# A gated linear recurrence and a max-out layer on one core: w_out loaded two rows to a partition, unit 0's gates in halves of heads, decays from sums of row pairs

## The chip, the core and the metric

The kernel runs on one core of a Trainium2 chip. The core has a matrix engine (TensorE, PE; its weight loads are listed apart as PEld), a vector engine (VectorE, DVE), a scalar engine (ScalarE, ACT), a general engine (GpSimd, POOL) and an engine that issues transfers (SyncE, SP). Each works through its own list of instructions in order and waits on semaphores. SBUF holds tiles of 128 partitions; PSUM has eight banks that TensorE writes. Times are device microseconds of one run.

## The reference

```
_attn: batch, n_heads, seq, head_dim = 4, 8, 768, 48
for t in range(S):
    state = alpha[:, :, t, :, None] * state + k[:, :, t] (outer) v[:, :, t]
    y[:, :, t] = q[:, :, t] @ state
x = y, heads side by side              # 3072 rows x 384
h1, h2 = x @ w1, x @ w2                # 384 x 1024 each
out = maximum(h1, h2) @ w_out          # 1024 x 384
```

All inputs and the output are fp32. Alpha lies between 0.8 and 1.0.

## The kernel before

**Units.** The 4 x 768 positions are cut into 12 units of 256 positions: unit u is batch u % 4, and its place in the sequence is u // 4. A unit has two chunks of 128 positions. `load(u)` brings alpha, k, q and v in; `gla(u)` computes the recurrence of the unit; `moe(u)` computes the layer behind it.

**The recurrence by chunks.** `ln` (ACT) takes the logarithm of alpha into `lg`, two positions (r = 0, 1) to a partition. `sums` (TensorE) multiplies `lg` by triangular matrices, which gives running sums within a chunk (`cs`, one PSUM bank to a chunk). For units 2 to 11 these matmuls use half of the array's rows ("tiled" in the plan); for units 0 and 1, the `TWO` units, they use full matrices `ti` and `ts`. `exps` has three parts: eight small TensorE matmuls per unit (`e_de`, line 494) that sum `lg` over groups of 32 partitions with the indicator `ind4`, for decays of whole half-chunks and chunks; exponentials of minus the sums (`em`, line 499) and of the sums (in place, line 501); and the exponential of the decays (`de`, line 504). `prep` multiplies k by `em` on POOL (`kn`, line 540) and q by the other on DVE (`qn`, line 542), and transposes both on TensorE (line 550, copied out as `qk` by DVE, line 558). `chunk` makes the scores (`e_p`, line 641, also tiled), masks them on DVE (`pt`, line 663), forms the new state `tm` (DVE, line 624) from k-v products (line 612), scales the former state by the decays into `sb` (POOL, line 599), and computes y from both (`e_y`, lines 672 and 675). y is copied out (`yc`, ACT, line 683), transposed (line 689) and stored as `xt` (DVE).

**The layer.** Instead of max(x w1, x w2) it computes x w2 + max(x (w1 - w2), 0). `weights` subtracts the weights on DVE (`w12`, line 439, four slices g of 256 columns) and casts `w_out` to `wo` (line 444; slices 0 and 1 on ACT, 2 and 3 on POOL). `w2_rows` casts w2 (`w2h`, ACT, line 412), transposes it and multiplies it by `wo` into `w2o` (line 429, 24 matmuls), so that x w2 w_out becomes one product with a 384 x 384 matrix. `moe(u)` makes four hidden products (`e_h`, line 729, one PSUM bank each), takes their ReLU into `gt` (ACT, line 740; for f2 = 1 from unit 3 on by DVE, line 737), and adds the output products (`e_o`, line 760) of `xt` with `w2o` and of `gt` with `wo`.

**The order of the work.** `Plan` is a list scheduler that runs while the program is built. Every step is given to it with an engine, a planned duration, what it reads and writes, and a key; PSUM banks are assigned on the way. At each planned moment an engine takes the ready step with the lowest key. The keys are ten times the unit plus offsets; `OFF0` shifts them for units 0 and 1. The resulting order of each engine is then fixed in the program. A change of one duration or key therefore can move other steps. Where the plan expects TensorE to be without work in the first 40 us, filler matmuls on `wsrc` (line 450) are placed.

**Transfers.** All loads are issued by SP in the order of `HEAD` and then unit by unit:

```
HEAD = 'k0 a0 a1 q0 v0 k1 q1 w20 w22 w21 v1 wo0 wo1 wo2 wo3 w11 w10 w13 w12'
```

Here `a0` is alpha of unit 0, `w20` is row block 0 of w2, `wo0` is slice 0 of w_out and `w11` is slice 1 of w1. The outputs are stored by ACT's queue.

Of the kernel before, what the change touches and what calls it, by code (L numbers as in the profile page):

```python
# [196 lines left out]
LATE = 2.5
# [5 lines left out]
JOIN_PP = -50  # L203
CS_UP = 2
RING = 3
OFF = {}
OFF0 = {'DVE:xt': -3.0, 'DVE:pt': -15.7, 'PE:op': 8.8, 'PE:hp': -8.2, 'ACT:yc': -9, 'PE:x': 6.7}
HEAD = 'k0 a0 a1 q0 v0 k1 q1 w20 w22 w21 v1 wo0 wo1 wo2 wo3 w11 w10 w13 w12'


# [1 line left out]
def kernel(  # L212
# [29 lines left out]
    def sbt(name, shape, dt, n=1):  # L242
        return [constp.tile(shape, dt, name=f"{name}{i}") for i in range(n)]
# [61 lines left out]
    add("DVE", c_warm, 0.25, writes=["wsrc"], key=-9)  # L305
    nc.scalar.preload_act_table_set("natural_log_exp_and_others")
    for i in range(2):
        add("DVE", lambda i=i: nc.vector.memset(LG[i], 0.0), 0.35, writes=[("lg", i)], key=-8)

    def c_t2():  # L310
        nc.gpsimd.memset(t2, 1.0)
# [58 lines left out]
    for i in range(4):  # L370
        add("DVE", lambda i=i: nc.vector.memset(SB[i], 0.0), 0.2, writes=[("sb", i)], key=-4)


    def load(u, what="akqv"):
        n, (b, cp) = u % NLD, (u % B, u // B)
        t0 = 256 * cp
        lat = 2.5 + max(0.0, min(LATE, LATE * (u - 1) / 3.0))
        ws = [({4: "w2f", 5: "w1f", 6: "wof"}[u], g) for g in range(3 if u == 4 else 4)] if u in (4, 5, 6) else []

        def pairs(dst, src, keys):  # L380
            add("SP", lambda: nc.sync.dma_start(  # L381
                out=dst.rearrange("p (h x) -> p h x", h=H),
                in_=src[b, :, t0 : t0 + 256, :].rearrange("h (p r) d -> p h (r d)", r=2)),
                1.26 if u in TWO else 1.5, writes=[*keys, *ws], key=-1, lat=lat)
# [15 lines left out]

    def load_w(m, g):
        fs = slice(256 * g, 256 * g + 256)
        if m == "2":
            dst, src, t = w2f[:, g, :], moe_w2[128 * g : 128 * g + 128, :], 1.36
        elif m == "1":
            dst, src, t = w1f[:, :, fs], moe_w1[:, fs].rearrange("(s p) f -> p s f", p=128), 1.15
        else:
            dst, src, t = wof[:, 2 * g : 2 * g + 2, :], moe_w_out[fs, :].rearrange("(s p) d -> p s d", p=128), 1.1
        add("SP", lambda: nc.sync.dma_start(out=dst, in_=src), t, writes=[(f"w{m}f", g)], key=-1, lat=2.5)  # L409

    def w2_rows(ds):
# [14 lines left out]
        y = f"wq{ds}"
        P.ps(y, 1, "w")
        for f in range(NF):
            add("PE", lambda f=f: nc.tensor.matmul(
                b32(y, DM), lhsT=w2T[:, f, 128 * ds : 128 * ds + 128], rhs=wo16[:, f, :],  # L430
                start=(f == 0), stop=(f == NF - 1)),
                0.162, reads=[("w2T", ds), ("wo16", f // 2)], writes=[y], key=KEY_WO)
        add("ACT", lambda: nc.scalar.copy(out=w2o[:, ds, :], in_=b32(y, DM)),
            0.38, reads=[y], writes=[("w2o", ds)], key=KEY_WO)

    def weights(g):
        fs = slice(256 * g, 256 * g + 256)
        eng, ns = ("POOL", nc.gpsimd) if g in W12_POOL else ("DVE", nc.vector)
        add(eng, lambda: ns.tensor_sub(out=w12[:, :, fs], in0=w1f[:, :, fs], in1=w2f[:, :, fs]),
            1.9 if g in W12_POOL else 0.95, reads=[("w1f", g), *(("w2f", ds) for ds in range(ND))],  # L440
            writes=[("w12", g)], key=KEY_W12)
        on = g in WO_ACT
        cp = nc.scalar.copy if on else nc.gpsimd.tensor_copy
        add("ACT" if on else "POOL", lambda: cp(  # L444
            out=wo16[:, 2 * g : 2 * g + 2, :], in_=wof[:, 2 * g : 2 * g + 2, :]),
            0.73 if on else 0.9, reads=[("wof", g)], writes=[("wo16", g)], key=KEY_W)
# [8 lines left out]
    def csv(u, i):  # L455
        return b32(("cs", u, i), DM).rearrange("p (h d) -> p h d", h=H)

    def ln(u):
        lg = LG[u % 2]
        add("ACT", lambda: nc.scalar.activation(  # L460
            out=lg[:, :, :, 0:D].rearrange("p r h d -> p h r d"), in_=AF[u % NLD], func=ACTF.Ln),
            0.82, reads=[("af", u % NLD)], writes=[("lg", u % 2)], key=10 * u)
        for i in range(2):
            P.ps(("cs", u, i), 1, "g")

    def e_cs(u):
        lg = LG[u % 2]
        if u in TWO:
            for i in range(2):
                for r in range(2):  # L470
                    nc.tensor.matmul(csv(u, i), lhsT=ts if r > i else ti, rhs=lg[:, r, :, 0:D],
                                     start=(r == 0), stop=(r == 1))
            return
        for r in range(2):
            for a in range(2):
                s = slice(64 * a, 64 * a + 64)
# [1 line left out]
                                 start=(r == 0), stop=(r == 1))  # L478

    def sums(u):  # L480
        by2 = u in TWO
        add("PE", lambda: e_cs(u), 0.65 if by2 else 0.33, reads=[("lg", u % 2), "tt" if by2 else "t2"],
            writes=[("cs", u, 0), ("cs", u, 1)], key=10 * u + (0 if by2 else CS_UP), tiled=not by2, join=10 * u + (0 if by2 else JOIN_CS))

    def exps(u):
        lg, de, k0 = LG[u % 2], DE[u % 8], 10 * u

        def dps():
            return bank(("cs", u, 0))[:, 384:400].rearrange("p (j m) -> p j m", j=HP)

        def e_de():
            for j in range(HP):
                for r in range(2):
                    nc.tensor.matmul(dps()[:, j, :], lhsT=pm(lg[:, r, 2 * j : 2 * j + 2, :]), rhs=ind4,  # L494
                                     start=(r == 0), stop=(r == 1))
        add("PE", e_de, 0.2, reads=[("lg", u % 2), "ind4"], writes=[("cs", u, 0)], key=k0)
        for i in range(2):
            em = (2 * u + i) % RING
            add("ACT", lambda i=i, em=em: nc.scalar.activation(out=EM[em], in_=csv(u, i), func=ACTF.Exp, scale=-1.0),  # L499
# [7 lines left out]
    def gla(u):  # L507
# [10 lines left out]
        if by2:  # L518
# [13 lines left out]
        def prep(i):  # L532
# [7 lines left out]
            add("POOL", lambda: nc.gpsimd.tensor_mul(out=kn[:, :, 0:D], in0=kin, in1=EM[m3]),  # L540
                0.95, reads=[*rk, ("em", m3)], writes=[("kn", m3)], key=kk)
# [33 lines left out]
        def chunk(a):  # L575
# [69 lines left out]
            elif a == 0:  # L645
# [204 lines left out]
```

## Time and profile before

| | us |
|---|---|
| median of 3 runs | 140.12 (139.96 to 141.34) |
| the profiled execution's own time | 140.14 |
| its span, first to last instruction | 138.0 |
| mean granted TensorE clock | 0.998 |
| TensorE busy | 132.0 |
| VectorE busy | 94.2 |
| ScalarE busy | 83.1 |
| GpSimd busy | 65.7 |
| bytes moved, in and out | 28.58 MB |

How the lines of the profile are read. In a timeline a line is a run of like instructions: start, time from the start of the first to the end of the last, engine, line of the code, operation, output <- input, shape, count, and in brackets the idle time of the engine before it and what ended that. Matmuls are pipelined, so the end of one lies after the start of the next; distances between starts say what a matmul costs. In a table by windows a line is a stretch, its length, the busy time of each engine with its instructions in brackets, TensorE's granted clock, the share of time in which the transfer engines were busy, and GB/s. In the row of slices each digit is the busy share of a fortieth of the span, in tenths.

### The profile page before, as it was taken

The numbers are of one execution on the slowest core, as the hardware profiler recorded it, in microseconds if no ns is written. First come the engines' busy times: TensorE is split into PE (matmuls) and PEld (weight loads), VectorE is DVE, ScalarE is ACT, GpSimd is POOL, SyncE is SP. The second block draws the span as 40 slices with busy tenths as digits, with TensorE's granted clock in tenths as the row PEclk, the third lists the DMA queues.
The fourth block names the chain that finished last, engine by engine and source line by source line (L and its number), as shares of the span: only waits on it lengthen the run. The fifth ranks groups of instructions, "written<-read, shape, count | busy, mean of one in ns | idle before, by whom it ended". The sixth has DMA issues, their size and how long they took to land.

```text
span 138.0 us, 4307 instructions
## 1 busy us (share of the span) xinstructions
PE 132.0 (96%) x1704; PEld 101.7 (74%) x1704; DVE 94.2 (68%) x199; ACT 83.1 (60%) x176; POOL 65.7 (48%) x127
## 2 busy tenths in 40 slices
PE   6698999999999999999999999999999999999991
PEld 6686985777768768678777877877777778687870
DVE  4936999932868847968977949948929759474300
ACT  3295895679364876565844845837737638245341
POOL 7458547206418159186482871844845817500000
PEclk9999999999999999999999999999999999999999
DMA  3999999989999999999989999999999130030113
GB/s 94 319 313 380 374 381 350 265 171 194 236 280 226 256 220 208 239 229 188 316 165 210 271 200 290 202 245 293 226 183 271 23 114 5 0 114 5 73 41 114
DMA packets 87427, 28.58 MB, mean 207 GB/s; under 512 B 81520, under 2 KB 86768, under 8 KB 87408
## 3 DMA queue, kind: packets, MB, share of 16 engines
q1 hardware_dynamic: 84240, 23.60, 72.9%
q10 hardware_dynamic: 3168, 4.72, 9.1%
q8 instruction: 13, 0.21, 0.6%
q14 instruction: 6, 0.05, 0.1%
HBM read 23.59 MB, written 4.72 MB: 205 GB/s over the span
## 4 chain that ended last, share of the span: by engine, by line
PE 79%; SPq 9%; DMA 6%; POOL 2%; issue 1%; ACT 0%; ACTq 0%
PE pb L760 31%; PE pb L729 23%; PE pb L550 6%; DMA ld<-in_moe_w_out_dram 6%; SPq L381 5%; PE pb L641 4%; SPq L409 4%; PE pb L675 3%; PE pb L689 3%; PE pb L477 3%; PE pb L672 3%; PE pb L612 2%; PE pb L494 2%; POOL sb L599 1%; POOL wo L444 1%
## 5 line engine op out<-in xcount | busy, mean ns | idle before, releaser
L760 PE MATMUL pb<-wo,gt 128*128 128x384 f16 (+2 forms) x200 | 39.1, 319 | 0.0
L540 POOL TENSOR_TENSOR kn<-ld,em 128x384 f16<-128x384 f32 x24 | 23.5, 1000 | 30.5 <-ACT em L499 26.7
L729 PE MATMUL pb<-xt,w 128*128 128x256 f16 x288 | 36.0, 272 | 0.0
L740 ACT ACTIVATE gt<-pb 128x512 f16<-128x512 f32 x39 | 23.1, 598 | 13.3 <-PE pb L729 12.2
L663 DVE TENSOR_TENSOR pt<-pb,u 128x512 f16<-128x512 f32 x48 | 29.8, 684 | 1.0 <-PE pb L641 0.7
L729 PEld LDWEIGHTS <-w 128*128 128x128 f16 x288 | 26.8, 98 | 3.7
L760 PEld LDWEIGHTS <-gt 128*128 128x128 f16 x200 | 17.7, 98 | 8.4
L599 POOL TENSOR_TENSOR sb<-tm,dd 64x192 f16<-64x192 f32 x40 | 20.7, 518 | 4.8 <-DVE tm L624 2.3
L768 ACT COPY os<-pb 128x384 f32<-128x384 f32 (+2 forms) x25 | 11.6, 468 | 18.8 <-PE pb L760 18.8
L558 DVE COPY qk<-pb 128x1024 f16<-128x1024 f16 x20 | 13.8, 691 | 11.6 <-ACT os L768 10.2
L542 DVE TENSOR_TENSOR qn<-ld,pb 128x384 f16<-128x384 f32 x24 | 12.4, 549 | 8.9 <-ACT pb L501 7.5
L760 PE MATMUL pb<-w2o,xt 128*128 128x384 f16 (+2 forms) x75 | 15.8, 319 | 0.0
L561 POOL CAST vc<-ld 128x384 f16<-128x384 f32 x20 | 10.0, 504 | 11.7 <-DMA ld<-in_v_dram 11.0
L499 ACT ACTIVATE em<-pb 128x384 f32<-128x384 f32 x24 | 10.8, 491 | 6.3 <-PE pb L477 6.3
L460 ACT ACTIVATE lg<-ld 128x768 f16<-128x768 f32 x12 | 10.2, 846 | 5.2 <-DVE qn L369 3.8
L683 ACT CAST yc<-pb 128x384 f16<-128x384 f32 x24 | 11.8, 491 | 2.5 <-PE pb L675 1.8
L698 DVE COPY xt<-pb 128x384 f16<-128x384 f16 x20 | 7.1, 356 | 6.8 <-PE pb L689 6.4
L624 DVE TENSOR_TENSOR tm<-pb,sb 64x192 f32<-64x192 f32 x32 | 11.3, 352 | 0.6
L675 PEld LDWEIGHTS <-pt 128*128 128x128 f16 x192 | 9.6, 96 | 2.2 <-issue 1.0
L450 PE MATMUL pb<-wsrc 128*128 128x128 f16 x125 | 9.9, 242 | 1.1 <-DVE wsrc L304 1.1
L501 ACT ACTIVATE pb<-pb 128x384 f32<-128x384 f32 x24 | 10.8, 489 | 0.0
L675 PE MATMUL pb<-vc,pt 128*128 128x48 f16 x160 | 9.6, 184 | 0.0
(79 smaller groups left out, 179.2 us busy)
## 6 DMA issues: line engine op xcount, KB each, us to landing
ld<-in_alpha_dram SPq DMA_DIRECT2D x12, 384.0 KB, 5.0
out_dram<-os ACTq DMA_DIRECT2D x11, 384.0 KB, 4.1
ld<-in_k_dram SPq DMA_DIRECT2D x20, 192.0 KB, 4.5
ld<-in_q_dram SPq DMA_DIRECT2D x20, 192.0 KB, 4.3
ld<-in_v_dram SPq DMA_DIRECT2D x20, 192.0 KB, 4.6
ld<-in_moe_w_dram SPq DMA_DIRECT2D x3, 512.0 KB, 6.1
ld<-in_moe_w_out_dram SPq DMA_DIRECT2D x4, 384.0 KB, 7.7
ld<-in_moe_w_dram SPq DMA_DIRECT2D x4, 384.0 KB, 8.3
```

Source lines behind the costliest of these rows:

```text
L540: add("POOL", lambda: nc.gpsimd.tensor_mul(out=kn[:, :, 0:D], in0=kin, in1=EM[m3]), 0.95, reads=[*rk, ("em", m3)], writes=[("kn", m3)], ke ...
L542: add("DVE", lambda: nc.vector.tensor_mul(out=qn[:, :, 0:D], in0=qin, in1=csv(u, i)), 0.5, reads=[*rq, ("cs", u, i)], writes=[("qn", m3)], ...
L558: add("DVE", lambda: nc.vector.tensor_copy(out=QK[m3], in_=b16(tp, 1024).rearrange("p (w j c) -> p w j c", w=2, j=HP)), 0.6, reads=[tp], w ...
L599: add("POOL", lambda r=r, e=e: nc.gpsimd.tensor_mul(out=sb[r, :, e], in0=TM[tmo][r], in1=dd[r, :].unsqueeze(2).to_broadcast([64, HP, D])), ...
L624: nc.vector.tensor_add(out=TM[tmi][r], in0=t[r, :, e], in1=sb[r, :, e])
L663: add("DVE", lambda e=e: nc.vector.tensor_mul(out=pt[:, e], in0=b32(pp[e], 512).rearrange("p (j c) -> p j c", j=HP), in1=uv.unsqueeze(1).t ...
L675: nc.tensor.matmul(t[:, 96 * j + D * e : 96 * j + D * e + D], lhsT=pt[:, e, j, :], rhs=vc[:, 2 * j + e, :], start=not has, stop=(e == 1) o ...
L683: add("ACT", lambda: nc.scalar.copy(out=yc, in_=b32(yp, DM)), 0.38, reads=[yp], writes=[("yc", ci % 2)], key=kk)
L729: nc.tensor.matmul(t[:, m, :], lhsT=w12[:, ds, f * 128 : f * 128 + 128], rhs=xt[:, ds].rearrange("p a c -> p (a c)"), start=(ds == 0), sto ...
L740: add("ACT", lambda g2=g2, v2=v2: nc.scalar.activation(out=g2, in_=v2(), func=ACTF.Relu), 0.48, reads=[x], writes=[("gt", u % 3, f2)], key ...
L760: nc.tensor.matmul(b32(x, c1 - c0), lhsT=l, rhs=r, start=first and y == 0, stop=last and y == len(ws) - 1)
L768: add("ACT", lambda m=m, x=x, c0=c0, c1=c1: nc.scalar.copy(out=os_[:, m, c0:c1], in_=b32(x, c1 - c0)), 0.06 + w / 1200.0, reads=[x], write ...
```

## The change

1. `w_out` is loaded with two neighbouring rows to a partition, so that a partition's part of a slice is one run of 3072 bytes and no longer two of 1536. This orders the hidden columns differently: column 256 g + 2 p + s is at partition p, place s. So the casts of w2 and the subtractions of the weights read their fp32 input at a step of two elements and write in the new order.
2. For unit 0, alpha is loaded in two transfers of four heads each, and the logarithm and the running sums are taken for each half. In both `TWO` units the sums of the second chunk (i = 1) now come first.
3. From unit 2 on, DVE adds the two positions of a partition (`ls`, 128 x 512 fp16), and `e_de` takes four matmuls on `ls` for its eight on `lg`.
4. The constants of the plan: slice 3 of `w12` is subtracted by POOL, all ReLUs are done by ACT (`RELU_DVE = 99`), and `KEY_WO` and `OFF0` are others.

`VX_DVE`, `KN_DVE` and `KN_HALF` are empty: the steps that they govern stay where they were.

```diff
-KEY_WO = 16
+KEY_WO = 21
-W12_POOL = ()
+W12_POOL = (3,)
-RELU_DVE = 3
+RELU_DVE = 99
+PAIR = 2
+SPLIT = (0,)
+KN_DVE = ()
+VX_DVE = ()
+PAIR_ON = 'DVE'
-OFF0 = {'DVE:xt': -3.0, 'DVE:pt': -15.7, 'PE:op': 8.8, 'PE:hp': -8.2, 'ACT:yc': -9, 'PE:x': 6.7}
+OFF0 = {'PE:hp': -6.7, 'ACT:yc': -18.0, 'PE:x': 6.7, 'PE:op': 9}
...
+    def halves(u):
+        return [(0, H // 2, 0), (H // 2, H, 1)] if u in SPLIT else [(0, H, 0)]
...
-                out=dst.rearrange("p (h x) -> p h x", h=H),
-                in_=src[b, :, t0 : t0 + 256, :].rearrange("h (p r) d -> p h (r d)", r=2)),
+                out=dst.rearrange("p (h x) -> p h x", h=H)[:, h0:h1],
+                in_=src[b, h0:h1, t0 : t0 + 256, :].rearrange("h (p r) d -> p h (r d)", r=2)),
...
-moe_w_out[fs, :].rearrange("(s p) d -> p s d", p=128), 1.1
+moe_w_out[fs, :].rearrange("(p s) d -> p s d", s=2), 0.98
...
-        add("ACT", lambda: nc.scalar.copy(out=w2h[:, ds, :], in_=w2f[:, ds, :]),
+        add("ACT", lambda: nc.scalar.copy(
+            out=w2h[:, ds, :].rearrange("p (g s x) -> p g s x", g=4, s=2),
+            in_=w2f[:, ds, :].rearrange("p (g x s) -> p g s x", g=4, s=2)),
...
-        add(eng, lambda: ns.tensor_sub(out=w12[:, :, fs], in0=w1f[:, :, fs], in1=w2f[:, :, fs]),
+        add(eng, lambda: ns.tensor_sub(
+            out=w12[:, :, fs].rearrange("p a (s x) -> p a s x", s=2),
+            in0=w1f[:, :, fs].rearrange("p a (x s) -> p a s x", s=2),
+            in1=w2f[:, :, fs].rearrange("p a (x s) -> p a s x", s=2)),
...
+        if u in TWO:
+            for h0, h1, y in halves(u):
+                for i in (1, 0):
+                    def e_cs2(i=i, h0=h0, h1=h1):
+                        for r in range(2):
+                            nc.tensor.matmul(csv(u, i)[:, h0:h1], lhsT=ts if r > i else ti,
+                                             rhs=LG[u % 2][:, r, h0:h1, 0:D], start=(r == 0), stop=(r == 1))
...
+        pair = u >= PAIR
+        ls = LS[u % 2]
+        if pair:
+            ns = nc.vector if PAIR_ON == "DVE" else nc.gpsimd
+            add(PAIR_ON, lambda: ns.tensor_add(out=ls, in0=lg[:, 0], in1=lg[:, 1]),
+                0.35 if PAIR_ON == "DVE" else 0.6, reads=[("lg", u % 2, 0)], writes=[("ls", u % 2)], key=k0)
...
             for j in range(HP):
-                for r in range(2):
-                    nc.tensor.matmul(dps()[:, j, :], lhsT=pm(lg[:, r, 2 * j : 2 * j + 2, :]), rhs=ind4,
-                                     start=(r == 0), stop=(r == 1))
+                hs = slice(2 * j, 2 * j + 2)
+                parts = [ls[:, hs, :]] if pair else [lg[:, r, hs, :] for r in range(2)]
+                for y, x in enumerate(parts):
+                    nc.tensor.matmul(dps()[:, j, :], lhsT=pm(x), rhs=ind4, start=y == 0, stop=x is parts[-1])
```

More of the change, by code (lines that the diff above doesn't have):

```diff
@@ L205 @@
 RING = 3
+PAIR = 2
+SPLIT = (0,)
+KN_DVE = ()
+VX_DVE = ()
+WO_PAIR = True
+KN_HALF = ()
+PAIR_ON = 'DVE'
 OFF = {}
-OFF0 = {'DVE:xt': -3.0, 'DVE:pt': -15.7, 'PE:op': 8.8, 'PE:hp': -8.2, 'ACT:yc': -9, 'PE:x': 6.7}
+OFF0 = {'PE:hp': -6.7, 'ACT:yc': -18.0, 'PE:x': 6.7, 'PE:op': 9}
 HEAD = 'k0 a0 a1 q0 v0 k1 q1 w20 w22 w21 v1 wo0 wo1 wo2 wo3 w11 w10 w13 w12'
@@ L250 @@
     LG = sbt("lg", [128, 2, H, 64], FP16, 2)
+    LS = sbt("ls", [128, H, 64], FP16, 2)
     KN = sbt("kn", [128, H, 64], FP16, RING)
@@ L307 @@
     for i in range(2):
-        add("DVE", lambda i=i: nc.vector.memset(LG[i], 0.0), 0.35, writes=[("lg", i)], key=-8)
+        add("DVE", lambda i=i: nc.vector.memset(LG[i], 0.0), 0.35, writes=[("lg", i, 0), ("lg", i, 1)], key=-8)
     def c_t2():
@@ L378, in load, with pairs @@
         ws = [({4: "w2f", 5: "w1f", 6: "wof"}[u], g) for g in range(3 if u == 4 else 4)] if u in (4, 5, 6) else []
-        def pairs(dst, src, keys):
+        def pairs(dst, src, keys, h0=0, h1=H):
             add("SP", lambda: nc.sync.dma_start(
-                out=dst.rearrange("p (h x) -> p h x", h=H),
-                in_=src[b, :, t0 : t0 + 256, :].rearrange("h (p r) d -> p h (r d)", r=2)),
-                1.26 if u in TWO else 1.5, writes=[*keys, *ws], key=-1, lat=lat)
+                out=dst.rearrange("p (h x) -> p h x", h=H)[:, h0:h1],
+                in_=src[b, h0:h1, t0 : t0 + 256, :].rearrange("h (p r) d -> p h (r d)", r=2)),
+                (1.26 if u in TWO else 1.5) * (h1 - h0) / H, writes=[*keys, *ws], key=-1, lat=lat)
         if "a" in what:
-            pairs(LD[n][:, 0, :], alpha, [("af", n)])
+            for h0, h1, y in halves(u):
+                pairs(LD[n][:, 0, :], alpha, [("af", n, x) for x in ((y,) if u in SPLIT else (0, 1))], h0, h1)
         rest = [x for x in (("k", "kf", KF, k), ("q", "qf", QF, q), ("v", "vf", VF, v)) if x[0] in what]
@@ L407, in load_w @@
         else:
-            dst, src, t = wof[:, 2 * g : 2 * g + 2, :], moe_w_out[fs, :].rearrange("(s p) d -> p s d", p=128), 1.1
+            dst, src, t = wof[:, 2 * g : 2 * g + 2, :], moe_w_out[fs, :].rearrange("(p s) d -> p s d", s=2), 0.98
         add("SP", lambda: nc.sync.dma_start(out=dst, in_=src), t, writes=[(f"w{m}f", g)], key=-1, lat=2.5)
     def w2_rows(ds):
-        add("ACT", lambda: nc.scalar.copy(out=w2h[:, ds, :], in_=w2f[:, ds, :]),
+        add("ACT", lambda: nc.scalar.copy(
+            out=w2h[:, ds, :].rearrange("p (g s x) -> p g s x", g=4, s=2),
+            in_=w2f[:, ds, :].rearrange("p (g x s) -> p g s x", g=4, s=2)),
             1.03, reads=[("w2f", ds)], writes=[("w2h", ds)], key=KEY_W)
@@ L459, in ln @@
         lg = LG[u % 2]
-        add("ACT", lambda: nc.scalar.activation(
-            out=lg[:, :, :, 0:D].rearrange("p r h d -> p h r d"), in_=AF[u % NLD], func=ACTF.Ln),
-            0.82, reads=[("af", u % NLD)], writes=[("lg", u % 2)], key=10 * u)
+        for h0, h1, y in halves(u):
+            add("ACT", lambda h0=h0, h1=h1: nc.scalar.activation(
+                out=lg[:, :, h0:h1, 0:D].rearrange("p r h d -> p h r d"), in_=AF[u % NLD][:, h0:h1], func=ACTF.Ln),
+                0.1 + 0.72 * (h1 - h0) / H, reads=[("af", u % NLD, y)], writes=[("lg", u % 2, x) for x in ((y,) if u in SPLIT else (0, 1))], key=10 * u)
         for i in range(2):
@@ L467, in e_cs @@
         lg = LG[u % 2]
-        if u in TWO:
-            for i in range(2):
-                for r in range(2):
-                    nc.tensor.matmul(csv(u, i), lhsT=ts if r > i else ti, rhs=lg[:, r, :, 0:D],
-                                     start=(r == 0), stop=(r == 1))
-            return
         for r in range(2):
@@ L480, in sums @@
     def sums(u):
-        by2 = u in TWO
-        add("PE", lambda: e_cs(u), 0.65 if by2 else 0.33, reads=[("lg", u % 2), "tt" if by2 else "t2"],
-            writes=[("cs", u, 0), ("cs", u, 1)], key=10 * u + (0 if by2 else CS_UP), tiled=not by2, join=10 * u + (0 if by2 else JOIN_CS))
+        if u in TWO:
+            for h0, h1, y in halves(u):
+                for i in (1, 0):
[3 more added lines that the diff above has]
+                                             rhs=LG[u % 2][:, r, h0:h1, 0:D], start=(r == 0), stop=(r == 1))
+                    add("PE", e_cs2, 0.325 * (h1 - h0) / H, reads=[("lg", u % 2, y), "tt"],
+                        writes=[("cs", u, i)], key=10 * u)
+        else:
+            add("PE", lambda: e_cs(u), 0.33, reads=[("lg", u % 2, 0), "t2"],
+                writes=[("cs", u, 0), ("cs", u, 1)], key=10 * u + CS_UP, tiled=True, join=10 * u + JOIN_CS)
     def exps(u):
@@ L489, in dps @@
             return bank(("cs", u, 0))[:, 384:400].rearrange("p (j m) -> p j m", j=HP)
+        pair = u >= PAIR
[4 more added lines that the diff above has]
+                0.35 if PAIR_ON == "DVE" else 0.6, reads=[("lg", u % 2, 0)], writes=[("ls", u % 2)], key=k0)
         def e_de():
             for j in range(HP):
[L493 to L496, printed above, removed]
+                hs = slice(2 * j, 2 * j + 2)
+                parts = [ls[:, hs, :]] if pair else [lg[:, r, hs, :] for r in range(2)]
+                for y, x in enumerate(parts):
+                    nc.tensor.matmul(dps()[:, j, :], lhsT=pm(x), rhs=ind4, start=y == 0, stop=x is parts[-1])
+        add("PE", e_de, 0.1 if pair else 0.2, reads=([("ls", u % 2)] if pair else [("lg", u % 2, y) for _, _, y in halves(u)]) + ["ind4"],
+            writes=[("cs", u, 0)], key=k0)
         for i in range(2):
@@ L523, in gla @@
                 s = slice(64 * a, 64 * a + 64)
-                add("POOL", lambda a=a, s=s: nc.gpsimd.tensor_copy(out=vx[s, a : a + 2], in_=v2[s]),
-                    0.9, reads=[("vf", n, a)], writes=[(vk, a)], key=k0 + 2.2)
+                on, ns = ("DVE", nc.vector) if 2 * u + a in VX_DVE else ("POOL", nc.gpsimd)
+                add(on, lambda a=a, s=s, ns=ns: ns.tensor_copy(out=vx[s, a : a + 2], in_=v2[s]),
+                    0.6 if on == "DVE" else 0.9, reads=[("vf", n, a)], writes=[(vk, a)], key=k0 + 2.2)
             for a in range(2):
@@ L539, in prep @@
             rq = [("qf", n, x) for x in ((0, 1) if by2 else (i,))]
-            add("POOL", lambda: nc.gpsimd.tensor_mul(out=kn[:, :, 0:D], in0=kin, in1=EM[m3]),
-                0.95, reads=[*rk, ("em", m3)], writes=[("kn", m3)], key=kk)
+            on, ns = ("DVE", nc.vector) if ci in KN_DVE else ("POOL", nc.gpsimd)
+            add(on, lambda: ns.tensor_mul(out=kn[:, :, 0:D], in0=kin, in1=EM[m3]),
+                0.52 if ci in KN_DVE else 0.95, reads=[*rk, ("em", m3)], writes=[("kn", m3)], key=kk)
             add("DVE", lambda: nc.vector.tensor_mul(out=qn[:, :, 0:D], in0=qin, in1=csv(u, i)),
@@ L653, in chunk @@
                     P.u = u
-                    add("PE", lambda: (e_p((0, 1)), e_cs(u + 1)), 0.76, reads=[*rd, ("lg", (u + 1) % 2), "t2"],
+                    add("PE", lambda: (e_p((0, 1)), e_cs(u + 1)), 0.76, reads=[*rd, ("lg", (u + 1) % 2, 0), "t2"],
                         writes=[*wr, ("cs", u + 1, 0), ("cs", u + 1, 1)], key=k0 + 4.5, tiled=True)
```

## The prediction

> **What bounds the kernel now.** I read the page's busy shares and slices first.
>
> ```profile
> PE 132.0 (96%) x1704; PEld 101.7 (74%) x1704; DVE 94.2 (68%) x199; ACT 83.1 (60%) x176; POOL 65.7 (48%) x127
> ...
> PE   6698999999999999999999999999999999999991
> ```
>
> A full TensorE row alone proves little, since filler matmuls on `wsrc` count as busy. So I cut the span by windows and looked up where the filler lies: its 125 matmuls (L450) all end before 19.2 us.
>
> ```profile
> 11.00:15.00 4.00, 3.45 (x77) 3.10 (x75) 2.85 (x6) 2.01 (x5) 3.06 (x6) 1.00 1.03 393
> 16.50:20.50 4.00, 4.00 (x85) 3.38 (x83) 3.91 (x8) 3.98 (x7) 1.83 (x3) 1.00 1.07 383
> 21.00:25.00 4.00, 3.90 (x33) 2.22 (x31) 3.71 (x9) 2.54 (x7) 3.27 (x4) 1.00 1.10 347
> 25.00:134.50 109.50, 109.50 (x1371) 83.15 (x1371) 75.05 (x147) 66.09 (x145) 49.98 (x94) 1.00 0.80 185
> ```
>
> From 25 to 134.5 us TensorE is never idle, with no filler: there every TensorE nanosecond saved or added moves the end, and other engines count only if they make it wait. Before 25 us the head is a relay of transfers (DMA share 1.0), DVE (full from 13 us) and POOL. The last relay, in order of time:
>
> ```profile
> 22.34 0.83 POOL L444 CAST wo<-ld 128x768 f16<-128x768 f32 x1 [0.16 <-DMA ld<-in_moe_w_out_dram]
> 22.54 2.27 PE L429 MATMUL pb<-wo,w2T 128*128 128x384 f16 x13
> ...
> 23.13 1.74 POOL L599 TENSOR_TENSOR sb<-tm,dd 64x192 f16<-64x192 f32 x2
> 23.54 0.96 DVE L439 TENSOR_TENSOR w<-ld,ld 128x768 f16<-128x768 f32 x1 [0.23 <-DMA ld<-in_moe_w_dram]
> ...
> 24.91 0.20 PE L672 MATMUL pb<-sb,qu 128*128 128x96 f16 x1
> ```
>
> Two `sb` multiplies take 1.74 us where their row's mean is 518 ns: the second started with the `w12` subtraction on DVE and ended 0.37 us after it. The chain of waits takes TensorE from there. In the steady part, two orders:
>
> ```profile
> 55.85 0.62 PE L641 MATMUL pb<-qk 48*128 48x128 f16 x16
> 56.40 0.50 PE L760 MATMUL pb<-wo,gt 128*128 128x384 f16 x2
> 56.74 0.82 PE L729 MATMUL pb<-xt,w 128*128 128x256 f16 x6
> 57.49 0.50 PE L477 MATMUL pb<-lg,t 64*128 64x384 f16 x4
> ```
>
> ```profile
> 84.00 0.62 PE L641 MATMUL pb<-qk 48*128 48x128 f16 x16
> 84.46 0.49 PE L477 MATMUL pb<-lg,t 64*128 64x384 f16 x4
> 84.88 0.35 PE L494 MATMUL pb<-ind,lg 128*128 128x4 f16 x8
> 85.10 1.47 PE L729 MATMUL pb<-xt,w 128*128 128x256 f16 x12
> ```
>
> Read starts, not durations. Eight decay matmuls (L494) cost 0.22 us; the scores (L641) cost 0.46 us before the sums (L477) and 0.55 before anything else, and the sums begin 0.09 us late behind a full-array group (six L729 take 6 x 0.109 = 0.66, so the gap ends at 57.49).
>
> [...] the eight weight loads of L494 begin at 84.88 and the next one at 85.08, 25 ns each. [...] DVE's subtraction kept its 0.95 us and POOL waited. [...] no instruction of before reads single elements at a step, so nothing here shows it. [...]
>
> **The change part by part**, on the profiled execution's 140.14 us (span 138.0 and 2.1 around it); the median, 140.12, is the same to 0.02.
>
> *Decay from pairwise sums.* In ten units (2 to 11) four decay matmuls replace eight. By starts four cost 4 x 25 = 0.10 us; the chain of waits, which charges ends, has 0.28 for eight, so 0.14 for four. Nothing hides them. I take 0.12: 10 x 0.12 = **-1.2 us** (bounds -1.0, -1.4).
>
> DVE gains ten `ls` additions of 512 fp16. [...] In the changed order an `ls` stands behind `tm` and ahead of four `pt`, where the ReLU (0.69 us, L737) stood. At 83.42 to 84.16 `tm` runs, TensorE wants the decay at 84.88: 0.72 us for it. So 0, either way, unless it is held. Queued behind it on DVE: the `pt` multiplies; behind the waiting decay on TensorE: hidden products. Its own input, the logarithm, is done 4 us earlier (88.81 for sums at 94.0). DVE ends lighter: 9 ReLUs x 0.692 = 6.2 us go[...].
>
> *Nine ReLUs to ACT*: 9 x 0.598 = 5.4 us on an engine busy 66 of 109.5. Units 0 to 2 already run all four there and TensorE stays full at 28 to 60 us. 0; if an exponential were late by one, 0.6 us per unit, for which the idle 0.94 us ahead of `em` at 84.99 is the cover.
>
> *Order.* The program's orders show scores and sums adjacent for two more pairs (units 3/4 and 4/5). Each saves 0.09 out and 0.09 in: 2 x 0.18 = **-0.36 us**.
>
> *Unit 0's halves.* Half of alpha lands about 0.6 us earlier (196 KB at 316 GB/s), two half logarithms end about 0.3 earlier. But ACT keeps unit 1's logarithm ahead of unit 0's first exponential, and that waits for a transfer until 7.11:
>
> ```profile
> 5.91 0.84 ACT L460 ACTIVATE lg<-ld 128x768 f16<-128x768 f32 x1 [3.83 <-DVE qn L369]
> ...
> 7.11 0.84 ACT L460 ACTIVATE lg<-ld 128x768 f16<-128x768 f32 x1 [0.36 <-DMA ld<-in_alpha_dram]
> ...
> 7.86 0.85 ACT L499 ACTIVATE em<-pb 128x384 f32<-128x384 f32 x2
> ```
>
> Besides, DVE waits for unit 1's q until 13.03. 0. The extra issue (0.4 us on SP's queue) precedes alpha 1 and every later load, but the transfers behind it are backlogged; uncovered it is 0.4.
>
> *w_out.* 1024 packets of 1536 B become 512 of 3072. The windows give 393 GB/s with 4096-B packets, 383 mostly at 1536, 347 mostly at 1024: the gain for 1.57 MB is 0.04 to 0.25 us; I take 0.15 and let `wo` and every later load land that much earlier.
>
> *Step-2 reads* of `w1f`/`w2f` in three ACT copies and four subtractions: [...] the upper bound, half rate, is a rival below.
>
> *The head's order.* Before `y` of unit 1's second chunk stand 20 instead of 24 `w2o` matmuls, then one hidden product, then the other four. DVE's work up to the first subtraction is the same sum, so it starts at about 23.4, again on top of the second `sb`: done at 24.35 + 0.37 = 24.72, and `y` at 24.76 instead of 24.91. TensorE, free at 24.15, waits. Then it owes what it had not done: 4 x 0.162 = 0.65, less three transposes already done (0.17), plus two planned fillers (0.11): 0.59 - 0.15 = **+0.44 us**. POOL's own subtraction (two times a 1.0 us row, 2.0) starts at 25.5, is held by DVE's last one (0.95) to 28.5; wanted at 28.95, so free. It stands behind both `sb` and ahead of unit 2's `vc`, whose data lands at 30.8. If the second `sb` gets through first, the head gains 0.4 instead.
>
> Sum: 140.14 - 1.2 - 0.36 + 0.44 = 139.02, so **139.0**.
>
> **Rivals.** *A, better head:* w_out lands 0.7 us sooner or `sb` wins against the subtraction; `y` at 24.2, head -0.4, decay at its upper bound: 140.14 - 1.4 - 0.36 - 0.4 = 138.0; middle 138.4. For: transfers bound this stretch. Against: 383 and 393 GB/s are close.
>
> *B, `ls` held behind POOL:* a `vc` cast (0.504 us) in the way, [...] 0.4 us stall. A cast lies near the scores at 55.71, none at 84; three or four units of ten give +1.3: 140.3. Against: POOL, not DVE, was held.
>
> *C, slower: the stride.* At half rate [...] the first ends 25.15, the second `sb` 25.5, the second subtraction 27.25, the third 29.75; POOL's, held all along, about 31.4, and the fourth hidden product starts at 31.6 instead of 28.95: 139.0 + 2.6 = 141.6. It makes the kernel slower from about 44% per element (1.16 of 2.65). [...]
>
> *D, the split does nothing* is in the forecast.
>
> **The numbers.** Forecast 0.50, A 0.25, B 0.13, C 0.12. Range 138.0 (A's bound) to 140.3 (B), leaving out most of C and little below. One per cent is 1.4 us, about what a measurement of this kernel tells from no change: faster takes A and 0.12 of the forecast, 0.37; slower is the larger half of C, 0.07; the same 0.56.
>
> **What would show it.** Decay matmuls x4 with 0.10 to 0.14 us between starts; TensorE without idle from 29 us; `em` of unit 0 still at 7.9 behind the second logarithm; the second `sb` stretched again and `y` near 24.8; copies of `w2h` at 1.05 and subtractions at 0.95. Idle ahead of the decay naming `ls` shows B; longer copies show C. A steady TensorE with new waits on ReLUs would make me wrong in a way not listed.

## The result and the profile after

The changed kernel took 144.19 us (median of 4 runs, 143.79 to 145.21) against 140.04 us for the kernel before (also of 4 runs; the 140.12 above is of three of them): 1.029 times the time of before, with a 95% interval of 1.020 to 1.037. The forecast was 139.0, the range 138.0 to 140.3. The profiled execution took 143.79 us, its span 141.8 against 138.0. Where a run lay more than 1.5% above the fastest of its kernel, the medians and ratios below leave it out.

First the page: busy shares and slices.

```profile
PE 132.4 (93%) x1675; PEld 102.8 (73%) x1675; DVE 93.8 (66%) x199; ACT 89.6 (63%) x186; POOL 68.6 (48%) x128
...
PE   7988999269999999999999999999999999999991
```

TensorE is as busy as before (132.4 to 132.0 us), but the row of slices has a 2 and a 6 in the eighth and ninth place, from about 25 to 32 us, where before there were only nines. The table by windows puts a size on the hole (columns as before).

```profile
21.00:25.00 4.00, 4.00 (x48) 2.54 (x43) 3.12 (x7) 3.10 (x7) 2.61 (x4) 1.00 1.09 355
25.00:28.00 3.00, 0.52 (x13) 0.41 (x11) 0.67 (x1) 0.71 (x2) 0.63 (x1) 1.00 0.96 247
28.00:31.00 3.00, 1.48 (x10) 0.90 (x10) 3.00 (x3) 1.08 (x2) 2.31 (x1) 1.00 1.00 196
33.00:138.00 105.00, 105.00 (x1292) 79.96 (x1291) 70.41 (x143) 69.58 (x149) 50.09 (x93) 1.00 0.77 178
```

Of the six microseconds from 25 to 31 TensorE works in two; from 33 us it is never idle. In the first three of the six DVE, ACT and POOL work for only 0.6 to 0.7 us each as well. The timeline of the same stretch, that part of it which answers to the relay shown of before:

```profile
22.75 0.83 POOL L461 CAST wo<-ld 128x768 f16<-128x768 f32 x1 [0.31 <-DMA ld<-in_moe_w_out_dram]
23.54 1.08 POOL L631 TENSOR_TENSOR sb<-tm,dd 64x192 f16<-64x192 f32 x2
24.99 0.21 PE L704 MATMUL pb<-sb,qu 128*128 128x96 f16 x1
...
27.34 0.96 DVE L453 TENSOR_TENSOR w<-ld,ld 128x768 f16<-128x768 f32 x1 [3.15 <-DMA ld<-in_moe_w_dram]
27.37 2.93 POOL L453 TENSOR_TENSOR w<-ld,ld 128x768 f16<-128x768 f32 x1 [2.76 <-DMA ld<-in_moe_w_dram]
28.35 0.83 PE L761 MATMUL pb<-xt,w 128*128 128x256 f16 x6 [2.83 <-DVE w L453]
28.48 2.64 DVE L453 TENSOR_TENSOR w<-ld,ld 128x768 f16<-128x768 f32 x1
31.18 0.83 PE L761 MATMUL pb<-xt,w 128*128 128x256 f16 x6 [1.35 <-DVE w L453]
31.79 0.96 DVE L453 TENSOR_TENSOR w<-ld,ld 128x768 f16<-128x768 f32 x1
```

The first subtraction of the weights starts at 27.34 and not at 23.54, behind a wait of 3.15 us for a transfer of w1. Two lines further down TensorE pays for it, 2.83 us, and then 1.35 us for a second subtraction that lasts 2.64 us. Both `sb` ran in 1.08 us, for 1.74 before; no subtraction ran beside them. The chain of waits goes through the same place:

```profile
18.57 8.64 DMA ld<-in_moe_w_dram
...
27.34 0.06 DVE w L453
```

That transfer, issued at 18.57 and landed at 27.21, is the last of the four slices of w1, not slice 1, which the first subtraction reads. The steady part is as forecast. Scores, sums and decay in it (starts in the first column):

```profile
61.20 0.62 PE L673 MATMUL pb<-qk 48*128 48x128 f16 x16
61.66 0.49 PE L489 MATMUL pb<-lg,t 64*128 64x384 f16 x4
62.09 0.25 PE L524 MATMUL pb<-ind,ls 128*128 128x4 f16 x4
62.20 1.46 PE L792 MATMUL pb<-wo,gt 128*128 128x384 f16 x8
```

Four decay matmuls take 0.11 us from start to start, for 0.22 with eight, and the sums follow the scores after 0.46.

### The profile page after: what moved, and what is told of

It reads as the page before. It is cut to its first block, busy times and chain, and to the rows that moved or that the text cites. A ratio compares the mean times of both kernels' runs of the same rounds, so it can differ in the third digit from the quotient of the medians.

```text
span 141.8 us, 4248 instructions
## 1 busy us (share of the span) xinstructions
PE 132.4 (93%) x1675; PEld 102.8 (73%) x1675; DVE 93.8 (66%) x199; ACT 89.6 (63%) x186; POOL 68.6 (48%) x128
## 4 chain that ended last, share of the span: by engine, by line
PE 76%; DMA 11%; SPq 7%; DVE 2%; issue 1%; ACT 0%; ACTq 0%; DVEq 0%
PE pb L792 30%; PE pb L761 22%; PE pb L582 6%; DMA ld<-in_moe_w_dram 6%; SPq L392 5%; DMA ld<-in_v_dram 5%; PE pb L673 4%; PE pb L707 3%; PE pb L721 3%; PE pb L489 2%; PE pb L704 2%; PE pb L644 2%; DVE w L453 2%; SPq L421 2%; PE pb L524 1%
## 5 line engine op out<-in xcount | busy, mean ns | idle before, releaser
L761 PE MATMUL pb<-xt,w 128*128 128x256 f16 x288 | 35.4, 272 | 4.2 <-DVE w L453 4.2
L772 ACT ACTIVATE gt<-pb 128x512 f16<-128x512 f32 x48 | 28.2, 602 | 12.7 <-PE pb L761 11.1
L792 PEld LDWEIGHTS <-gt 128*128 128x128 f16 x200 | 17.2, 97 | 8.3 <-issue 0.6
L478 ACT ACTIVATE lg<-ld 128x768 f16<-128x768 f32 (+1 forms) x13 | 10.4, 803 | 5.0 <-DMA ld<-in_alpha_dram 4.5
L467 PE MATMUL pb<-wsrc 128*128 128x128 f16 x132 | 11.5, 251 | 1.1 <-DVE wsrc L312 1.1
L467 PEld LDWEIGHTS <-wsrc 128*128 128x128 f16 x132 | 10.0, 115 | 1.2 <-DVE wsrc L312 1.0
```

The source lines that it names most:

```text
L467: nc.tensor.matmul(PB[b][:, 0:128], lhsT=wsrc, rhs=wsrc, start=True, stop=True)
L761: nc.tensor.matmul(t[:, m, :], lhsT=w12[:, ds, f * 128 : f * 128 + 128], rhs=xt[:, ds].rearrange("p a c -> p (a c)"), start=(ds == 0), sto ...
L772: add("ACT", lambda g2=g2, v2=v2: nc.scalar.activation(out=g2, in_=v2(), func=ACTF.Relu), 0.48, reads=[x], writes=[("gt", u % 3, f2)], key ...
L792: nc.tensor.matmul(b32(x, c1 - c0), lhsT=l, rhs=r, start=first and y == 0, stop=last and y == len(ws) - 1)
```

## Where the wait comes from

The wait is in the program, and it can be read there. Two programs with the same order on every engine, which differ only in how w1 is stored (both with w_out in two rows and step-2 reads, the last two kernels of this section), have these waits ahead of the four subtractions, in their order ("slice 1" on the right of a colon is the transfer of that slice of w1, "w2 (3)" the transfers of the three row blocks of w2):

```
w1 stored slice by slice     w1 stored as before, slices interleaved
slice 1: w2 (3), slice 1     slice 1: w2 (3), slices 0, 1, 2 and 3
slice 0: slice 0             slice 0: nothing more
slice 3: slice 3             slice 3: nothing more
slice 2: slice 2             slice 2: nothing more
```

In the layout of before, a row of 1024 columns of `w1f` holds a piece of each slice, so from its first element to its last a slice reaches over pieces of the other three. With plain reads each subtraction still waits for its own slice (the first starts at 23.54 in the kernel before and at 23.41 in `e10_plain` below); with reads at a step of two elements the first waits for all (26.83 in `e13_step`). Interleaved storage and stepped reads are both needed. By what rule the waits are put in, these three cases don't show.

The changed kernel's first subtraction waits as in the right column, and so does its subtraction on POOL.

**Theory W**: this wait is the loss. **Theory T**: a part of it comes from later transfers in the head, because of the halves. The first experiments take both apart.

`e1_exact`, the changed kernel with w1 stored slice by slice:

```diff
-    w2f, w1f = (LD[i].rearrange("p a x -> p (a x)").rearrange("p (s f) -> p s f", s=ND) for i in (4, 5))
+    w2f = LD[4].rearrange("p a x -> p (a x)").rearrange("p (s f) -> p s f", s=ND)
+    w1f = LD[5].rearrange("p a x -> p (a x)").rearrange("p (g s f) -> p g s f", g=4, s=ND)
...
-            dst, src, t = w1f[:, :, fs], moe_w1[:, fs]...
+            dst, src, t = w1f[:, g], moe_w1[:, fs]...
...
-            in0=w1f[:, :, fs].rearrange("p a (x s) -> p a s x", s=2),
+            in0=w1f[:, g].rearrange("p a (x s) -> p a s x", s=2),
```

> The changed kernel with w1 kept slice after slice in its SBUF tile, so that the four slices are disjoint runs; same orders, same instructions. Theory W (the strided reads made the program wait, for all four w1 slices, ahead of the first subtraction): the first subtraction starts near 24.2 us instead of 27.3, TensorE's 4.2 us of waits on w12 shrink to at most 1, time 140.2 to 140.8. Rival S (the step of two elements is slow by itself): subtractions and waits stay long, 143 or more.

Measured: 139.98 us (18 of 20 runs; the median of all is 140.18, which the later expectations use), 0.999 of before (0.997 to 1.001). So the whole loss went with the storage of one tile. The runs spread widely, from 139.20 to 141.07 within the 18, so this median is known to about 0.3 us. The timeline:

```profile
24.69 0.95 DVE L454 TENSOR_TENSOR w<-ld,ld 128x768 f16<-128x768 f32 x1
25.83 0.99 DVE L454 TENSOR_TENSOR w<-ld,ld 128x768 f16<-128x768 f32 x1
26.95 2.16 POOL L454 TENSOR_TENSOR w<-ld,ld 128x768 f16<-128x768 f32 x1 [0.94 <-DMA ld<-in_moe_w_dram]
27.79 2.14 DVE L454 TENSOR_TENSOR w<-ld,ld 128x768 f16<-128x768 f32 x1 [0.31 <-DMA ld<-in_moe_w_dram]
29.98 2.79 PE L762 MATMUL pb<-xt,w 128*128 128x256 f16 x24 [0.18 <-DVE w L454]
```

No transfer is waited for ahead of the first subtraction, and of 4.2 us that TensorE waited for `w12` 0.18 are left. Subtractions at a step of two took 0.95 us on DVE, so rival C, half rate, is out.

`e2_wait`, the kernel before with one added copy of one element, never used, which makes the first subtraction wait for the slice that lands last:

```diff
...
+        def e_sub():
+            if g == 1:
+                nc.vector.tensor_copy(out=late[:, 0:1], in_=w1f[:, 2, 600:601])
+            ns.tensor_sub(out=w12[:, :, fs], in0=w1f[:, :, fs], in1=w2f[:, :, fs])
...
```

> The kernel before with one added DVE copy of one element ahead of the first subtraction, from the w1 slice that lands last: the wait alone, no stride. Theory W: the first subtraction starts near 26.8 us instead of 23.5, the hidden products follow it, 142 to 142.8. Rival S: less than 0.5 over the kernel before, since DVE and TensorE would find other work.

Measured: 144.39 us (142.97 to 144.71, 4 runs), 1.028 of before (1.024 to 1.032). The wait alone, in the kernel before, makes the loss; it is more than expected, for a reason told in the last section.

`e13_step`, the last kernel run, asks whether the part of the change on w_out brings the wait by itself. It is the kernel before with only that part (two rows to a partition, step-2 reads, w1 stored as before), the right column of the table:

```diff
-moe_w_out[fs, :].rearrange("(s p) d -> p s d", p=128), 1.1
+moe_w_out[fs, :].rearrange("(p s) d -> p s d", s=2), 0.98
...
+            in0=w1f[:, :, fs].rearrange("p a (x s) -> p a s x", s=2),
```

> The kernel before with only w_out two rows to a partition and the step-2 reads, w1 stored as before, slices interleaved; every engine's order is that of the version that stored w1 slice by slice (140.49). Theory W (interleaved slices and a step-2 read together make the first subtraction wait for all four slices): it starts when the last slice has landed, near 26.7 in place of 23.3, and TensorE waits for it: 143.5, 142.8 to 144.9. Rival (the wait costs only together with POOL's subtraction or the late head of the halves): below 141.5.

Measured: 144.23 us (143.21 to 145.19, 4 runs), 1.027 (1.021 to 1.033). Its timeline:

```profile
26.83 0.96 DVE L441 TENSOR_TENSOR w<-ld,ld 128x768 f16<-128x768 f32 x1 [3.53 <-DMA ld<-in_moe_w_dram]
27.85 0.83 PE L734 MATMUL pb<-xt,w 128*128 128x256 f16 x6 [3.12 <-DVE w L441]
```

Neither POOL's subtraction nor the halves are in this kernel, and the loss is the whole one.

`e9_rows` is the left column: the same part of the change, with w1 slice by slice (`w1f[:, g]` as in `e1_exact`).

> The kernel before with only w_out two rows to a partition, its step-2 reads, and w1 stored slice by slice so that each subtraction waits for its own slice. Prediction's steps: landing 0.15 earlier or nothing, copies of w2 on ACT 1.13 in place of 1.05 us (measured in the changed kernel), subtractions unchanged at 0.95: 139.9 to 140.2, no difference that can be measured. Rival (the longer copies of w2 delay its transposes in the head): 140.3 to 140.6, with TensorE's w2 transposes about 0.1 to 0.25 later.

Measured: 140.49 us, 1.0034 (1.0021 to 1.0047): 3.7 us less than `e13_step` with the same orders, but 0.46 more than before, on the rival's side. The copies of w2 took 1136 ns for 1046. Whether they cause the 0.46 is taken up with `e10_plain` below.

## What the other parts cost

**The halves.** `e4_split`: the kernel before with unit 0's alpha, logarithm and sums in halves, and the second chunk's sums first, and nothing else of the change.

```diff
+SPLIT = (0,)
...
+            for h0, h1, y in halves(u):
+                pairs(LD[n][:, 0, :], alpha, [("af", n, x) for x in ((y,) if u in SPLIT else (0, 1))], h0, h1)
```

> The kernel before with unit 0's alpha, logarithm and sums in halves, and nothing else of the change. As predicted: no difference (140.0). Theory T (the two half transfers slow the first ones behind them: unit 1's logarithm began 0.5 us later in the changed kernel): 0.4 to 0.7 us slower, with unit 1's logarithm near 7.6 us and unit 1's q near 13.6.

Measured: 141.22 us, 1.0074 (1.0045 to 1.0102): +1.1.

`e11_onealpha` keeps the half logarithms and sums but loads alpha in one transfer:

```diff
-            for h0, h1, y in halves(u):
-                pairs(LD[n][:, 0, :], alpha, [("af", n, x) for x in ((y,) if u in SPLIT else (0, 1))], h0, h1)
+            pairs(LD[n][:, 0, :], alpha, [("af", n, x) for x in (0, 1)])
```

> The kernel before with unit 0's logarithm and sums in halves of heads, but alpha of unit 0 in one transfer; with alpha in two it took 141.22. Theory X (the cost is in the transfers: two of 192 KB in place of one of 384 KB delay all later loads): 140.0 to 140.3, q of unit 1 awaited until about 13.0. Rival Y (the cost is in the half logarithms and sums and in the order that they bring): 140.9 to 141.4, although the transfers land as before.

Measured: 140.07 us, 1.0001 (0.9984 to 1.0018). Its orders are those of `e4_split` but for one exponential on ACT and the places and number of filler matmuls, so the cost is in the transfers. SP's issues (start, time that the issue took), first of `e4_split`:

```profile
1.27 1.67 SPq L392 DMA_DIRECT2D ld<-in_alpha_dram  x3
...
5.47 1.87 SPq L392 DMA_DIRECT2D ld<-in_k_dram  x1
7.38 1.15 SPq L392 DMA_DIRECT2D ld<-in_q_dram  x1
```

and of `e11_onealpha`:

```profile
1.29 1.83 SPq L392 DMA_DIRECT2D ld<-in_alpha_dram  x2
...
5.55 1.15 SPq L392 DMA_DIRECT2D ld<-in_k_dram  x1
6.75 1.15 SPq L392 DMA_DIRECT2D ld<-in_q_dram  x1
```

The third issue of alpha cost SP no time. Behind it an issue took 1.87 us for 1.15, so unit 1's q was issued 0.63 later, and DVE's wait for it ended at 13.65 for 12.78 (13.03 in the kernel before). From 4 to 8 us the transfers moved 307 GB/s in place of 325 (319 before). Why two transfers of 192 KB slow the queue more than one of 384 KB stays open. One issue was long in the kernel before too, 1.52 us for q of unit 0, and the long one isn't always the same: 1.87 us for k of unit 1 here, 1.60, 2.08 and 2.29 for v of unit 0 in `e1_exact`, the changed kernel and `e3_eight`. That would fit the wide spread of `e1_exact`, where the middle half of the runs spans 1.1 us, and of `e4_split`, 0.8, against 0.1 to 0.3 in `e11_onealpha`, `e6_dve` and `e12_joins`, which load alpha in one transfer; with one trace of each kernel it isn't shown. The changed kernel moved 286 GB/s in those 4 us, and on ACT it shows

```profile
4.85 0.52 ACT L478 ACTIVATE lg<-ld 128x384 f16<-128x384 f32 x1 [2.77 <-DMA ld<-in_alpha_dram]
5.97 0.52 ACT L478 ACTIVATE lg<-ld 128x384 f16<-128x384 f32 x1 [0.60 <-DMA ld<-in_alpha_dram]
7.61 0.84 ACT L478 ACTIVATE lg<-ld 128x768 f16<-128x768 f32 x1 [1.11 <-DMA ld<-in_alpha_dram]
8.36 0.85 ACT L529 ACTIVATE em<-pb 128x384 f32<-128x384 f32 x2
```

Unit 0's first half starts a microsecond earlier than the whole did, and the first `em`, which stands behind unit 1's logarithm, half a microsecond later.

`e5_whole` takes the halves out of `e1_exact` (`SPLIT = ()`).

> The changed kernel with w1 stored slice by slice, and unit 0's alpha, logarithm and sums whole again (SPLIT empty); all else as in that version (140.18). Theory T (the halves cost 1.0, measured alone on the kernel before): 139.2, 139.0 to 139.5, and q of unit 1 lands about 0.6 earlier again, DVE's wait for it ending near 13.1. Rival (in the changed order the late q is hidden behind the new order of the head, and the halves cost nothing there): 140.0 to 140.3.

Measured: 139.20 us, 0.9942 (0.9928 to 0.9957), 0.78 less than `e1_exact`, and 13.03 again for the end of DVE's wait. The halves cost in both orders, 0.8 and 1.1 by medians that spread, and without them and without the wait the change beats the kernel before.

**Rows and steps.** `e10_plain` has the order of `e5_whole` on every engine, but w_out in its former rows, w1 stored as before, slices interleaved, and no stepped reads:

```diff
-moe_w_out[fs, :].rearrange("(p s) d -> p s d", s=2), 0.98
+moe_w_out[fs, :].rearrange("(s p) d -> p s d", p=128), 0.98
...
-            in0=w1f[:, g].rearrange("p a (x s) -> p a s x", s=2),
+            in0=w1f[:, :, fs],
```

> The version with unit 0 whole and exact waits, with w_out loaded in its former row order (1536-byte runs) and no step-2 reads, w1 stored as before; the planned duration of the w_out transfers stays at 0.98, so that every engine's order is the same as in that version (139.2). Theory R (rows and stride alone cost nothing; the 0.46 that they cost on the kernel before came from TensorE's new order, one join of scores and sums lost and one filler matmul late, 0.18 + 0.06 by the trace): within 0.15 of it, 139.05 to 139.35, with copies of w2 at 1.05 on ACT. Rival S (the copies of w2, 0.09 longer each, delay the head): 138.7 to 138.95. Rival P (the longer runs of w_out do save transfer time): 139.4 or more.

Measured: 139.09 us, 0.9934 (0.9921 to 0.9946), the fastest median of all kernels here. In this order rows and steps are worth nothing that the runs tell apart: 0.11 us, within the intervals. The transfers did run faster with 3072-byte runs, 399 GB/s for 374 from 18 to 20 us, and DVE's last wait for w1 ended at 26.67 for 26.85; nothing behind it needed that. So the longer copies do not cost 0.46 by themselves. `e9_rows` changed a planned duration too (0.98 for 1.1), which moved the plan: one pair of scores and sums fewer stands together, and one filler matmul stands behind 25 us. By the trace's prices that is 0.24. A part can still be the copies in that order: its chain of waits passes through the second one (15.79 to 16.93 us), and TensorE's third group of w2 transposes starts at 18.50 for 18.38, 0.12 later. The rest is open.

**The decay.** `e3_eight` is `e1_exact` with the eight decay matmuls in the places of the four. It keeps the additions, whose results aren't read.

```diff
-                parts = [ls[:, hs, :]] if pair else [lg[:, r, hs, :] for r in range(2)]
+                parts = [lg[:, r, hs, :] for r in range(2)]
```

> Like e1_exact, but the decay takes eight matmuls on lg again, in the same places; the addition still runs and nobody reads it. Price of the saving by itself: 1.0 to 1.4 us slower than e1_exact if TensorE sets the steady part, as the prediction had it; no difference if something else does.

Measured: 141.08 us, 1.0067 (1.0047 to 1.0087), 1.1 more than `e1_exact`. Four matmuls fewer in ten units are worth 1.1 by the starts as well (0.11 a unit), though both medians are of kernels that spread.

**POOL's subtraction.** `e6_dve` is `e5_whole` with `W12_POOL = ()`.

> The version with w1 slice by slice and unit 0 whole, and the fourth subtraction of the weights on DVE again in place of POOL. Theory H (POOL's subtraction and DVE's third one hold each other for 2.1 us, but that is hidden behind what TensorE still owes): within 0.2 of the version with POOL, and four subtractions of 0.95 to 1.0 each. Rival (the holding delays the last group of hidden products): 0.3 to 0.8 faster than the version with POOL.

Measured: 140.26 us, 1.06 more than `e5_whole`: neither case. The subtractions took about 0.95 us each, as expected, and the holding was gone, but the order that came with it is a worse one. The scores of one unit stand no longer beside sums, and TensorE waits once in the steady part, for an `xt` on DVE:

```profile
54.24 0.82 PE L762 MATMUL pb<-xt,w 128*128 128x256 f16 x6 [0.66 <-DVE xt L731]
```

0.66 and 0.18 for the join make 0.84 of the 1.06. The run doesn't say what the holding costs. In `e5_whole` the starts say it:

```profile
26.67 2.01 DVE L454 TENSOR_TENSOR w<-ld,ld 128x768 f16<-128x768 f32 x1 [0.40 <-DMA ld<-in_moe_w_dram]
27.45 1.14 PE L793 MATMUL pb<-w2o,xt 128*128 128x384 f16 x6
28.73 2.79 PE L762 MATMUL pb<-xt,w 128*128 128x256 f16 x24
```

The subtraction that POOL's holds, 2.01 us for 0.95, ends at 28.68, and the hidden products start 0.05 later. The six output matmuls ahead of them take 1.28 us from start to start, where six take 0.98 in the changed kernel (32.12 to 33.10). So the holding costs about 0.3 us there, and about 0.1 in `e10_plain` (1.09 us). TensorE's idle time doesn't show it, since the modelled end of the matmuls lies over most of it.

**The head's constants.** `e7_head` is `e5_whole` with the constants of before in the head (`KEY_WO = 16`, `OFF0`, `W12_POOL = ()`).

> The version with w1 slice by slice and unit 0 whole, and the head's constants of before (KEY_WO 16, OFF0 of before, all subtractions on DVE); ReLUs all on ACT, pairwise sums and w_out in two rows kept. By the prediction's step on the head's order (+0.44): 0.4 faster than the version with the new constants, so about 138.8 if that gives 139.2. Rival (the new constants gain in the head, as they were worked out for the earlier w_out): 0.3 or more slower than it, 139.5 or above.

Measured: 139.15 us, 0.9935 (0.9921 to 0.9949), the same as `e5_whole`. Its scores and sums stand together in 6 units, against 8. By the price of 0.18 that is 0.36 more, so its head would be about 0.4 better.

`e12_joins` tried to have both: `e10_plain` with the former `KEY_WO` and `OFF0`, and POOL's subtraction.

> The version with unit 0 whole, rows and strides as before the change, with the former KEY_WO and OFF0 but the fourth subtraction on POOL and all ReLUs on ACT: in its program scores and sums stand together in 7 units, against 6 with all subtractions on DVE. By the price of a join (0.18) and two more filler matmuls behind 25 us (0.055 each): 0.1 below the version with the former constants and rows (139.15), about 139.05 (138.8 to 139.3). Rival (POOL's subtraction and DVE's hold each other and delay the last hidden products in this order): 139.5 or more.

Measured: 139.87 us, 0.9999 (0.9987 to 1.0011), 0.8 above the expectation, although scores and sums stand together in 7 units. Its trace shows one wait of TensorE of 0.30 us behind 25 us (for `xt`, at 44.6) and none for a subtraction. In the head it shows one of 0.44 us for a copy of w2 (at 15.21), which `e10_plain` doesn't have; what that does to the end wasn't worked out. Joins alone don't rank orders.

## Why the prediction was wrong

Worked as differences of medians, the 4.15 us are:

| from | to | us |
|---|---|---|
| before (139.99) | `e10_plain`: decay sums, order, constants | -0.90 |
| `e10_plain` | `e5_whole`: rows and steps | +0.11 |
| `e5_whole` | `e1_exact` (139.98): halves | +0.78 |
| `e1_exact` | changed kernel: the wait | +4.21 |

The sum, 4.20, differs from 4.15 because the kernel before had medians of 139.99 to 140.09 beside the different runs.

*Step-2 reads.* **This step failed.** The prediction priced the reads as a data path, at 0; no trace of before showed that price. For DVE it was right: an unheld subtraction took 0.95 us with the step (`e1_exact`) and without it (before). For ACT's copies (1134 ns for 1046) and POOL's subtraction (2.16 us for 1.81) it was not quite right, small beside what came. What a changed access pattern does to the waits was not asked. The prediction listed no added wait, and the program had one: the first subtraction waited for four slices in place of one, started at 27.34 in place of 23.54, and that cost 4.2 us. Rival C's 141.6 lay nearer, and the sign named for C, longer copies, did show; but its mechanism, subtractions at half rate, did not. Its times at half rate were the author's estimate and not shown.

*The head's order.* "It starts at about 23.4" failed with it: 27.34. The second `sb` wasn't held, and `y` started at 24.99 (forecast 24.76). Where the wait and the halves are out, the step was good: in `e10_plain` the second `sb` ends at 24.73 and `y` starts at about 24.8. There the sums of unit 2 start at 31.21,

```profile
31.21 0.50 PE L486 MATMUL pb<-lg,t 64*128 64x384 f16 x4
```

and in the kernel before at 30.94:

```profile
30.94 0.50 PE L477 MATMUL pb<-lg,t 64*128 64x384 f16 x4
```

Two more output matmuls were done by then before (2 x 0.163), so `e10_plain` is 0.27 + 0.33 = 0.60 behind, about 0.1 of it by the holding told above, for the forecast's 0.44.

*POOL's subtraction* "held by DVE's last one", "free": failed. POOL's subtraction, started at 27.37 with DVE's first one already running (27.34 to 28.30), took 2.93 us for 2.16 in `e1_exact`, and DVE's next, started at 28.48 while POOL's ran to 30.30, took 2.64 for 0.95. The prediction took POOL's wait in the trace of before, the one case, in which DVE had started first (23.54, `sb` at 23.70), for the rule. "Free" was 0.1 to 0.3 us short in `e10_plain` and `e5_whole`, by the starts above.

*Unit 0's halves*, "0": failed, +0.8 to +1.1. That ACT keeps unit 1's logarithm ahead of the first exponential was right, and so the gain was nil; "the transfers behind it are backlogged" was wrong: DVE's wait for unit 1's q ended 0.6 us later (13.66 for 13.03).

*Decay*, -1.2: right; 0.11 for 0.12 a unit by starts, 1.1 between the medians. *Order*, -0.36: two more joins were there. Together: `e10_plain`, 0.60 behind at unit 2's sums, ends 0.9 earlier by span (137.1), so the steady part gains 1.5 for the forecast's 1.56. In the changed kernel TensorE is full from 33 us. That the additions `ls` cost nothing rested on the author's estimate of their time, which no trace of before shows, and so did rival B's stall. They took 0.43 us (median of ten in the changed kernel). Some took longer, up to 1.25 us, but TensorE had no idle time for it, so the stall didn't come. No wait for the nine more ReLUs on ACT shows either.

*w_out*, 0.15 earlier: 0.18 by the wait for w1's last slice, and of no use. Its bounds, 0.04 to 0.25, don't follow from the rates beside them: 393 for 383 GB/s is 0.10 us for 1.57 MB.

The forecast of 139.0 describes `e10_plain` (139.09) and `e5_whole` (139.20): what it counted was about right, and what it set to 0, the wait and the halves, cost five.

## What to carry to other kernels

When an edit changes the pattern in which an instruction reads a buffer that several transfers fill, list the waits of that instruction in the built program before and after: the price of the read itself says nothing about them. A tile that is loaded in pieces can be stored piece by piece; here that alone took the wait away (first subtraction at 24.69 for 27.34). A transfer cut in two to start sooner is to be judged by when the transfers behind it land.

## What the runs showed of the hardware

**Of two subtractions that overlapped, the one started later took longer.** In six kernels POOL's subtraction was running when one of DVE's started, and each time DVE's ended 0.82 us after POOL's, whenever it had started: POOL 30.30, 29.11, 28.67, 27.86, 27.61 and 27.59, DVE 31.12, 29.93, 29.49, 28.68, 28.43 and 28.41. They took 1.58 to 2.64 us; where none of POOL's had started before them, DVE's took 0.94 to 1.09, mostly 0.95. For `e10_plain`, whose reads have no step:

```profile
25.80 1.81 POOL L452 TENSOR_TENSOR w<-ld,ld 128x768 f16<-128x768 f32 x1 [1.06 <-DMA ld<-in_moe_w_dram]
26.85 1.58 DVE L452 TENSOR_TENSOR w<-ld,ld 128x768 f16<-128x768 f32 x1 [0.64 <-DMA ld<-in_moe_w_dram]
```

Where DVE's had started first, POOL's took 2.93 us (changed kernel) and 2.33 (`e3_eight`), for 2.16 in `e1_exact` and `e5_whole`. With step-2 reads POOL's took 2.16 us for 1.81; DVE's showed no such difference (0.95 for 0.95).

**A wait of three microseconds cost more than itself in some runs.** After TensorE's idle 3 us in `e13_step` the granted clock fell, in the table by windows:

```profile
25.00:28.00 3.00, 0.15 (x2) 0.15 (x3) 1.14 (x2) 0.00 (x0) 0.00 (x0) 1.00 0.77 166
28.00:31.00 3.00, 3.00 (x29) 2.37 (x28) 3.00 (x5) 1.46 (x3) 0.71 (x1) 0.61 1.01 199
```

Here the runs of one kernel differ by it: with a mean clock of 1.0 `e13_step` took 143.21 and 143.61, with 0.988 144.85 and 145.19; `e2_wait`, granted 0.56 from 28 to 30 us in its trace, took 142.97 with 1.0 and 144.32 to 144.71 with 0.985 to 0.988. That is the excess over the expectation of `e2_wait`: its one run at full clock lies 0.2 above the expected 142.8. The changed kernel has it too, 143.79 and 144.03 with 1.0, 144.34 with 0.988 and 145.21 with 0.976, so a few tenths of its loss of 4.15 are the clock's. In all, 7 of the 12 runs of these three kernels had a mean clock of 0.988 or less, of the 107 runs of the other kernels tried here one, and of 92 of the kernel before beside them one. The profiled execution of the changed kernel, idle for 2.83 and 1.35 us, kept its clock. When such a wait costs the clock and when not stays open.
